# Moving single steps between engines in a fused top-k attention and gated-MLP kernel whose order is written out step by step

## The chip, the core and the metric

The kernel runs on one core of one Trainium2 chip. A core has TensorE (PE in the profile; its weight loads stand as PEld), VectorE (DVE), ScalarE (ACT), GpSimd (POOL) and SyncE (SP), which only issues DMAs here. Each engine works its own instruction queue in order; semaphores join the queues. The metric is the device time of one execution in microseconds.

## What is computed

```python
def _attn_ref(q, k, v):                 # (4, 8, 576, 64) each
    scores = np.matmul(q, k.transpose(0, 1, 3, 2)) / np.sqrt(64)
    kth = np.partition(scores, -32, axis=-1)[..., -32:-31]
    scores = np.where(scores >= kth, scores, -1e9)
    attn = np.exp(scores - np.max(scores, axis=-1, keepdims=True))
    attn = attn / (np.sum(attn, axis=-1, keepdims=True) + 1e-09)
    return np.matmul(attn, v)
def _moe_ref(x, w_in, w_out):           # x (2304, 512), w_in (512, 2048)
    h = x @ w_in
    return (h / (1.0 + np.exp(-1.702 * h))) @ w_out
def _moe2_ref(x, w1, w2, w3, w_out):    # d_ff 1024
    return ((x @ w1) * (x @ w2) @ w3) @ w_out
```

Attention keeps the 32 largest scores of each row; its output, with the heads side by side, goes through the two MLPs. The weights come as 64-bit floats, q, k and v as 32-bit floats.

## The kernel before

**Tiling.** The 2304 rows are 18 tiles of 128. A tile has 8 heads; then `tile_end` scales the tile's attention output and `moe` takes it through both MLPs. Tiles 4 and 13 hold rows of two batches, so their attention matmuls are made in two parts of 64 rows. Every operand of a product is split into two 16-bit halves, hi (rounded) and lo (what the rounding left), and each product is three matmuls: hi by hi, hi by lo, lo by hi (`product_op`, L669 to L671, 512 columns each).

**A head** (`head`): scores on TensorE (L903) into one of two PSUM tiles `s_ps`; four rounds of MAX8 (L925) and three of MATCH_REPLACE8 (L928) on VectorE find the 32nd largest; the bias `nbs` (L935, on GpSimd or VectorE); ScalarE cuts (L943) and takes exp (L946), which frees the score tile; the half `a hi` (`f_hi`, L952, ScalarE) and the difference `a lo` (L955 and L956, GpSimd); a DMA transpose; the product with v (`f_av`, L970) for each pair of heads, 9 matmuls a head, the first five with the hi halves of the softmax, the last four with the lo halves; `x0` (L1011) and `x1` (L1015) take it out of PSUM.

**The weights.** 72 blocks of 128 by 512 are loaded as 64-bit words and put together (`load64`): the low byte `w low` (L520, ScalarE), the sign `w sign` (L525 on GpSimd or L530 on ScalarE), the main word `w main` (L533, ScalarE, into PSUM), `w join` (L537, VectorE). Then Gram matmuls give a scale for each matrix (`l2_scale`, L564), and the blocks are split: `split_back` (hi at L606, back through TensorE, lo at L612) or `split_pe` (scaled on TensorE at L624, hi at L627, subtracted at L630, lo at L633 on ScalarE or L636 on VectorE). Five matrices follow one another through the same SBUF space: w4 and w3 (multiplied together into `w34`), w_in, w_out, then w1 and w2.

**q, k, v** are scaled by a factor for each row of q and each pair of heads of k and v: maximum or sum of absolute values, then three small VectorE steps of `f_pow2` (L773 to L775; the second masks the number down to a power of two), then halves (`split_op`: hi at L449 ScalarE, L452 VectorE or L466 GpSimd; lo at L459 VectorE or L462 and L463 GpSimd).

**The order.** Every step is an `Op` given to `Order.op`, with the engines that could do it (`alts`), the steps it depends on, and the buffers that it takes (`acq`) and gives back (`rel`). `PLAN` is a packed table with one number for each step: a rank in 13 bits and the chosen engine in 3. `Order.run` writes the steps out. In the kernel before it goes through modelled time: at each moment each free engine takes, of the steps that are ready and find their buffers, the one of lowest rank. The order thus written is fixed in the program; nothing is decided on the chip. `od.two` marks VectorE steps that the planner keeps apart from GpSimd's.

Of the kernel before, what the change touches and what calls it, by code (L numbers as in the profile page):

```python
# [34 lines left out]
class Op:  # L35
    __slots__ = ("alts", "fn", "prio", "acq", "rel", "left", "users", "ready", "end", "eng", "lat", "tag", "seq", "done", "start", "why", "data", "after")


class Order:

    GAP = {"T": 0.25, "V": 0.16, "A": 0.16, "G": 0.1, "D": 0.05}
    SAME = {"T": 0.0, "V": 0.11, "A": 0.12, "G": 0.1, "D": 0.25}
    DMA = 2.1

# [6 lines left out]
    def two(self, f):  # L54


        self.both.add(f)
        return f
# [4 lines left out]
    def op(self, alts, due, deps=(), env=None, acq=(), rel=(), tag="", lat=None, data=0.6, after=None):  # L63
        o = Op()
        o.after = after
        rank, k = self.plan[len(self.ops)]
        o.alts, o.prio, o.lat, o.data = [(*alts[k][:3], 0.0)], 0.2 * rank, lat, data
        o.acq = [(a, env, a) if isinstance(a, str) else a for a in acq]
        o.rel = [(a, env, a) if isinstance(a, str) else a for a in rel]
        o.left, o.users, o.ready, o.end, o.why = 0, [], 0.0, None, None  # L70
        o.tag, o.seq, o.done = tag, len(self.ops), False
        for d in deps:
            if d is not None:
                d.users.append(o)
                o.left += 1
        self.ops.append(o)
        return o

    def run(self, log=None):
        engs = "TVAGD"  # L80
        free = dict.fromkeys(engs, 0.0)
        lock = moved = 0.0
        used = dict.fromkeys(engs, 0.0)
        cand = {e: [] for e in engs}
        events = [0.0]
        for o in self.ops:
            if o.left == 0:
                for a in o.alts:
                    cand[a[0]].append((o, a, 0.0))
        n = 0  # L90
        ends = []
        now = 0.0
        while n < len(self.ops):
            if not events:
                left = [(o.tag, o.prio, [a for a, _, _ in o.acq if not self.pools[a]]) for o in self.ops if not o.done and o.left == 0]
                raise RuntimeError(f"nothing can go at {now}: {left}")
            now = heapq.heappop(events)
            while events and events[0] <= now:
                heapq.heappop(events)
            while ends and ends[0][0] <= now:  # L100
                _, _, o = heapq.heappop(ends)
                for u in o.users:
                    u.left -= 1
                    u.why = o
                    same = len(u.alts) == 1 and u.alts[0][0] == o.eng
                    u.ready = max(u.ready, o.end + (self.SAME[o.eng] if same else self.GAP[o.eng]))
                    if u.left == 0:
                        for a in u.alts:
                            r = u.ready + a[3]
                            cand[a[0]].append((u, a, r))  # L110
                            heapq.heappush(events, r)
            for e in engs:
                if free[e] > now:
                    continue
                best, rank = None, None
                for c in cand[e]:
                    o, a, r = c
                    if o.done or r > now or (o.after is not None and not o.after.done):
                        continue
                    both = e == "G" or (e == "V" and a[2] in self.both)  # L120
                    mine = (o.prio + (LOCK * max(lock - now, 0.0) if both else 0.0), o.seq)
                    if best is not None and mine >= rank:
                        continue
                    ok = True
                    for name, _, _ in o.acq:
                        if not any(s[0] <= now for s in self.pools[name]):
                            ok = False
                            break
                    if ok:
                        best, rank = c, mine  # L130
                if best is None:
                    continue
                o, a, _ = best
                cand[e] = [c for c in cand[e] if not c[0].done and c[0] is not o]
                o.done, o.eng = True, e
                wait = []
                for name, env, key in o.acq:
                    s = min(self.pools[name], key=lambda x: x[:2])
                    self.pools[name].remove(s)
                    env[key] = s[2]  # L140
                    wait.append((s[0], name, s[1]))
                o.start = now
                a[2]()
                cost = a[1]
                if e == "G" or (e == "V" and a[2] in self.both):
                    cost += max(lock - now, 0.0)
                    lock = now + cost
                free[e] = now + cost
                used[e] += cost
                o.end = now + cost  # L150
                if e == "D":
                    moved = max(moved, now) + o.data
                    o.end = max(o.end, moved) + (self.DMA if o.lat is None else o.lat)
                for name, env, key in o.rel:
                    t = o.end + self.GAP[e]
                    self.pools[name].append((t, o.seq, env[key]))
                    heapq.heappush(events, t)
                heapq.heappush(ends, (o.end, o.seq, o))
                heapq.heappush(events, o.end)
                heapq.heappush(events, free[e])  # L160
                if log is not None:
                    log.append((now, free[e], e, o.tag, o.seq, o.ready, o.why.seq if o.why else None, wait))
                n += 1
        return now, used
# [21 lines left out]
    'c-jru1B2zf0szpqX&W|alDpQ}voo`{ZQHhuZ*AMQZQHhO+q>_be{l@MF<b)~*dPWs0!C`1xM3R5@C@IOhBA^HX^r$o$^vPOaKko&j8G%Yh%};%7$echY'  # L186
    '-BW&j0{Feqq0%esBY9SY8my7CPvKy^^EpLHlwc5z-VMNH(DC)jIKscqis-!paI4~<BD<3xNST#o*1u;&&JcB=Rx0%hQ=D>uyNElWt=f?7=I0AelV=yw+'
    '1n#naoUO#+n(;qGm}mi`l?zY;rTv%xdN|^O;4=(q<L2m02pdoT-i6MuDKBMrp$`k{PLt2qV^@Mx2oll*Pzygc#L~+D2oesR4|1Mz9fW#2doMVdM(RXB0'
    'N_8qJJWMn|KI!Hi5sRwJj8$H;GVGP(uzG5Q-tj6udIV}dcwC}{LD{xe1x>x>G<Tw_sCax;Tj)|g_<4BBEGGpZOXjkQ5_%_in}<EC*hD6JW4?l7Q9gQLw'
    '%<_zPD@hhmI+01Nh>@xNT#hcm9B(s`XE4Y){#hh$BGk}@LEM!hKej5LRYMS-TNVA|>!t88zGZV}*X2sx^W_vTWnZwK*T*<6qmNUv5m5dff8>6$)-RNQT'  # L190
# [99 lines left out]
def plan():  # L290
    words = array.array("H", zlib.decompress(base64.b85decode("".join(PLAN))))
    return [(w & 8191, w >> 13) for w in words]
# [1007 lines left out]
```

## Time and profile before

| | |
|---|---|
| median of 3 runs | 1070.26 us (1066.76 to 1072.64) |
| the profiled execution's own time | 1068.41 us |
| its span, first to last instruction | 1066.6 us |
| mean granted TensorE clock | 0.957 |
| data read from HBM / written | 52.43 MB / 4.72 MB |

The busy share of an engine is a mean over the span. A recorded matmul ends later than the next one begins, so TensorE's busy time says that it had something under way, not that it ran at its peak. A wait is put down to the last semaphore that came. The granted clock is that of TensorE; 1.00 is 2.4 GHz.

### The profile page before, as it was taken

The page shows a single profiled execution, that of the slowest core. Times are in us where ns is not written, and L with a number is a line of the kernel's source. Part 1 is how long each engine was busy: PE and PEld are TensorE (multiplying, and loading weights), DVE is VectorE, ACT ScalarE, POOL GpSimd, SP SyncE. Part 2 cuts the span into 40 slices and gives each one's busy share as a digit, 9 for nine tenths or more (in the row PEclk, how much of TensorE's full clock was granted, in tenths as well). Part 3 has the DMA queues.
Part 4 walks back from the last instruction along what each step waited for, and adds up shares of the span by engine and source line. Part 5 has one row for each costly group of instructions (what it writes and reads, how often), then busy time and mean ns, then how long its engine had stood idle before and what let it go on. Part 6 is the DMA issues. An engine that isn't in the chain of part 4 may idle for free.

```text
span 1066.6 us, 18717 instructions
## 1 busy us (share of the span) xinstructions
PE 973.6 (91%) x5824; PEld 505.5 (47%) x5824; DVE 933.6 (88%) x2127; ACT 810.3 (76%) x1556; POOL 719.1 (67%) x1060
## 2 busy tenths in 40 slices
PE   3757898589689999999999999999999999999997
PEld 1333454344344545455555554555455555555543
DVE  4798898989788899999999999999999999999421
ACT  7897868989688868778878887788777867768432
POOL 1355533847576767889798898889789666656510
PEclk7767999769999999999999999999999999999999
DMA  9979977969764748876769678577685847645622
GB/s 260 291 181 236 248 143 187 273 124 199 185 127 88 134 94 149 147 138 136 143 119 169 120 130 164 118 146 134 132 143 106 158 95 135 114 94 95 114 50 69
DMA packets 428740, 156.96 MB, mean 147 GB/s; under 512 B 406624, under 2 KB 414816, under 8 KB 428640
## 3 DMA queue, kind: packets, MB, share of 16 engines
q1 hardware_dynamic: 428640, 155.78, 71.3%
q8 instruction: 45, 0.74, 0.3%
q14 instruction: 55, 0.45, 0.1%
HBM read 52.43 MB, written 4.72 MB: 54 GB/s over the span
## 4 chain that ended last, share of the span: by engine, by line
PE 52%; DVE 14%; DMA 11%; ACT 8%; POOL 8%; issue 5%; SPq 2%; POOLq 0%; ACTq 0%; DVEq 0%
PE mm L669 13%; PE mm L671 13%; PE mm L670 13%; DVE m8s L925 6%; DVE wsb L928 5%; PE mm L970 5%; DMA tsb<-hsb 4%; PE s_ps L903 4%; PE mm L624 2%; DMA wout<-in_moe_w_in_dram 1%; POOL hlb L956 1%; POOL hsb L463 1%; DVE win L612 1%; POOL fsb L1119 1%; ACT ysb L946 1%
## 5 line engine op out<-in xcount | busy, mean ns | idle before, releaser
L925 DVE MAX8 m8s<-wsb 128x8 f32<-128x576 f32 x432 | 322.9, 754 | 4.3
L928 DVE MATCH_REPLACE8 wsb<-m8s,wsb 128x576 f32<-128x576 f32 x288 | 213.8, 743 | 0.0
L669 PEld LDWEIGHTS <-tsb 128*128 128x128 f16 x1072 | 105.0, 98 | 135.1 <-DMA tsb<-hsb 22.3
L956 POOL TENSOR_TENSOR hlb<-ysb,hlb 128x512 f16<-128x512 f32 x144 | 166.7, 1157 | 0.0
L669 PE MATMUL mm<-w,tsb 128*128 128x512 f16 x432 | 163.9, 380 | 2.7 <-DMA tsb<-hsb 2.4
L671 PEld LDWEIGHTS <-tsb 128*128 128x128 f16 x1072 | 105.3, 98 | 127.8 <-issue 2.2
L671 PE MATMUL mm<-w,tsb 128*128 128x512 f16 x432 | 163.7, 379 | 0.0
L670 PE MATMUL mm<-w,tsb 128*128 128x512 f16 x432 | 163.7, 379 | 0.0
L670 PEld LDWEIGHTS <-tsb 128*128 128x128 f16 x1072 | 105.2, 98 | 113.7 <-issue 8.6
L669 PE MATMUL mm<-wout,tsb 128*128 128x512 f16 x352 | 134.7, 383 | 11.6 <-DMA tsb<-hsb 9.8
L943 ACT ACTIVATE s_ps<-s_ps,m8s 128x576 f32<-128x576 f32 x144 | 102.7, 713 | 43.8 <-DVE m8s L925 38.6
L670 PE MATMUL mm<-wout,tsb 128*128 128x512 f16 x352 | 134.5, 382 | 0.0
L671 PE MATMUL mm<-wout,tsb 128*128 128x512 f16 x352 | 134.4, 382 | 0.0
L946 ACT ACTIVATE ysb<-s_ps,nbs,asm 128x576 f32<-128x576 f32 x144 | 119.8, 832 | 8.3 <-POOL nbs L935 3.2
L925 DVE MAX8 m8s<-s_ps 128x8 f32<-128x576 f32 x144 | 108.9, 757 | 17.8 <-PE s_ps L903 15.1
L669 PE MATMUL mm<-win,tsb 128*128 128x512 f16 x288 | 110.0, 382 | 6.0 <-DMA tsb<-hsb 3.3
L670 PE MATMUL mm<-win,tsb 128*128 128x512 f16 x288 | 109.9, 381 | 0.0
L671 PE MATMUL mm<-win,tsb 128*128 128x512 f16 x288 | 109.7, 381 | 0.0
L903 PE MATMUL s_ps<-kts,qts 128*128 128x288 f16 (+1 forms) x640 | 97.9, 294 | 12.5 <-ACT ysb L946 10.0
L928 DVE MATCH_REPLACE8 wsb<-m8s,s_ps 128x576 f32<-128x576 f32 x144 | 107.7, 748 | 0.0
L952 ACT CAST hlb<-ysb 128x576 f16<-128x576 f32 x144 | 97.2, 675 | 13.1 <-DMA ats<-hlb 12.1
L955 POOL TENSOR_TENSOR hlb<-ysb,hlb 128x64 f16<-128x64 f32 x144 | 44.5, 309 | 90.1 <-ACT hlb L952 88.5
(199 smaller groups left out, 1835.7 us busy)
## 6 DMA issues: line engine op xcount, KB each, us to landing
w<-in_moe_w_dram SPq DMA_DIRECT2D x16, 512.0 KB, 6.9
wout<-in_moe_w_in_dram SPq DMA_DIRECT2D x16, 512.0 KB, 5.0
wout<-in_moe_w_out_dram SPq DMA_DIRECT2D x16, 512.0 KB, 4.6
qts<-qts SPq DMA_DIRECT2D x36, 128.0 KB, 2.6
out_dram<-fsb SPq DMA_DIRECT2D x18, 256.0 KB, 2.4
w<-in_moe_w_out_dram SPq DMA_DIRECT2D x8, 512.0 KB, 5.0
psb<-in_moe_w_dram SPq DMA_DIRECT2D x8, 512.0 KB, 4.5
tsb<-in_moe_w_dram SPq DMA_DIRECT2D x8, 512.0 KB, 4.6
```

The lines of the kernel that those rows point to most:

```text
L669: nc.tensor.matmul(o, a[:, i, :], hi, start=(first and i == 0), stop=False)
L670: nc.tensor.matmul(o, a[:, i, :], lo, start=False, stop=False)
L671: nc.tensor.matmul(o, a[:, 4 + i, :], hi, start=False, stop=(last and i == 3))
L903: nc.tensor.matmul(E["sp"][r : r + n, i], qe[q_][:, h, r : r + n], kt[:, j, i * HS : (i + 1) * HS], start=k_ == 0, stop=k_ == 1,)
L925: nc.vector.max(out=E["m8"][:, 8 * i : 8 * i + 8], in_=E["sp"] if i == 0 else E["w"])
L928: nc.vector.match_replace(out=two(E["w"]) if i == 0 else E["w"], in_to_replace=E["m8"][:, 8 * i : 8 * i + 8], in_values=E["sp"] if i == 0 ...
L943: nc.scalar.activation(E["sp"], E["sp"], AF.Prelu, bias=E["m8"][:, TOPK - 1 : TOPK], scale=-1.0, alpha=1.0 / FAR)
L946: nc.scalar.activation(two(E["y"]), E["sp"], AF.Exp, bias=E["nb"], scale=nesc)
L952: nc.scalar.copy(hl()[:, 0:S], E["y"])
L955: nc.gpsimd.tensor_tensor(hl()[:, S : S + SR], E["y"][:, SM:S], hl()[:, SM:S], op=ALU.subtract)
L956: nc.gpsimd.tensor_tensor(hl()[:, S + SR : 2 * S], E["y"][:, 0:SM], hl()[:, 0:SM], op=ALU.subtract)
L970: nc.tensor.matmul(heads_av()[r : r + n, j_], e["at"][:, i, r : r + n], v2[:, j_, blk, :], start=(i == 0), stop=(i == 8))
```

## The change

- **Engines to choose from.** Steps that had one engine get others: `w low` GpSimd; `w hi` of `split_back` VectorE and GpSimd; `w hi` of `split_pe`, `w34 hi`, `x0`, `he`, `x2 hi`, `a copy`, `b copy` and `o` VectorE; `a hi` and `th1` VectorE and GpSimd.
- **Scales.** The masking step of `f_pow2` goes (now `f_unit`): 50 VectorE steps fewer, 5182 steps for 5232.
- **The product with v.** The two halves of v change places in their tile, and the last four of a head's nine matmuls read 65 columns (the hi half and the ones column) where they read 130; the first five read 129. 640 of the 1440 matmuls of L970 are narrowed.
- **Order.** `Order.run` writes the steps out in the strict order of their ranks; modelled times only choose which of several free buffers a step gets. The durations that it holds are new. `PLAN` is new.

Unpacked, the two plans choose these engines (steps whose choice differs):

| step | before | after |
|---|---|---|
| `w low` | 72 A | 35 A, 37 G |
| `w sign` | 60 G, 12 A | 44 G, 28 A |
| `w hi` | 72 A | 55 A, 17 G |
| `w lo` | 42 V, 30 A | 35 V, 37 A |
| `a hi` | 144 A | 101 A, 40 G, 3 V |
| `x0` | 72 A | 57 A, 15 V |
| `th1` | 72 A | 53 A, 14 G, 5 V |
| `he` / `a copy` / `b copy` | 68 / 36 / 34 A | 6 / 6 / 2 of them V |
| `x2 hi` / `w34 hi` / `o` | 18 / 8 / 18 A | 3 / 1 / 1 of them V |
| `nb` | 85 G, 59 V | 80 G, 64 V |
| `g lo` / `p lo` on V (rest G) | 11 / 12 | 3 / 7 |
| `g hi` / `p hi` on V | 9 / 6 | 5 / 3 |
| `kvr hi` on V / on G | 7 / 9 | 2 / 14 |
| `q lo`, `kv lo`, `kvr lo` on V | 3, 13, 9 | 1, 12, 8 |

Here A is ScalarE, V VectorE, G GpSimd. Of the 37 `w low` that move to GpSimd, 27 stand in the first 124 us of the trace of before, 3 between 124 and 190 and 7 between 190 and 332; of the 40 `a hi`, 16 stand before 332 us. The steps that stay on their engine keep nearly their order: 51% of TensorE's, 57% of the DMAs and 66 to 70% of the other engines' stand at another place among them, by 1.0 to 1.5 places in the mean and by 29 at most.

```diff
-        return now, used
+        for o in sorted(self.ops, key=lambda o: o.rank):
+            e, cost, fn, _ = o.alts[0]
+            assert o.after is None or o.after.end is not None
...
+            fn()
...
-        lo = act(0.65, due, f_low, deps=[ld], tag="w low")
+        def f_low_g():
+            b3 = E[raw_pool].bitcast(U8).rearrange("p (c e) -> p c e", e=8)[:, :, 3]
+            low = dst.bitcast(U16).rearrange("p (c two) -> p c two", two=2)[:, :, 0]
+            nc.gpsimd.tensor_scalar(low, b3, 1.0 / 32, -15.5 / 32, op0=ALU.mult, op1=ALU.add)
+
+        lo = op([("A", 0.65, f_low, 0.0), ("G", 0.75, f_low_g, 0.0)], due, deps=[ld], tag="w low")
...
+        def f_hi_g():
+            nc.gpsimd.tensor_scalar(hi(), src(), sc, 1.0, op0=ALU.mult, op1=ALU.mult)
...
-    def f_pow2(inv, sc, src):
+    def f_unit(inv, sc, src):
         return [
             lambda: nc.vector.tensor_scalar(inv, src(), TINY, 2.0 ** -14, op0=ALU.max, op1=ALU.mult),
-            lambda: nc.vector.tensor_scalar(inv.bitcast(U32), inv.bitcast(U32), 0x7F800000, None, op0=ALU.bitwise_and),
             lambda: nc.vector.reciprocal(sc, inv),
         ]
...
+                        c0 = 0 if i < 5 else D
                         nc.tensor.matmul(
-                            heads_av()[r : r + n, j_], e["at"][:, i, r : r + n], v2[:, j_, blk, :], start=(i == 0), stop=(i == 8)
+                            heads_av()[r : r + n, j_, c0 : P + 1], e["at"][:, i, r : r + n], v2[:, j_, blk, c0 : P + 1],
+                            start=(i == 0), stop=(i == 8),
                         )
...
-        hi = act(0.58, due + 6, f_hi, deps=[y], env=E, acq=["hl"], tag="a hi", after=last_of.get("a hi"))
+        def f_hi_g():
+            nc.gpsimd.tensor_scalar(hl()[:, 0:S], E["y"], 1.0, 1.0, op0=ALU.mult, op1=ALU.mult)
+
+        hi = op([("A", 0.58, f_hi, 0.0), ("V", 0.42, od.two(f_hi_v), 0.0), ("G", 0.75, f_hi_g, 0.0)], due + 6, deps=[y], env=E, acq=["hl"], tag="a hi", after=last_of.get("a hi"))
```

## Rows read from the trace of the kernel before

**Rows 1.** The page: busy us, share of the span and instructions of each engine.
```profile
PE 973.6 (91%) x5824; PEld 505.5 (47%) x5824; DVE 933.6 (88%) x2127; ACT 810.3 (76%) x1556; POOL 719.1 (67%) x1060
```
**Rows 2.** By stretch: length; PE, PEld, DVE, ACT, POOL busy (instructions); PEclk; DMA share, GB/s.
```profile
0.00:124.00 124.00, 77.42 (x387) 40.75 (x388) 97.83 (x235) 103.87 (x203) 55.17 (x102) 0.77 0.95 244
124.00:190.00 66.00, 62.33 (x346) 30.83 (x345) 61.95 (x138) 54.41 (x101) 26.70 (x41) 1.00 0.77 178
190.00:264.00 74.00, 55.36 (x345) 30.95 (x343) 68.64 (x142) 66.80 (x118) 51.31 (x70) 0.82 0.88 194
264.00:331.00 67.00, 53.56 (x319) 26.91 (x317) 55.58 (x133) 51.03 (x95) 43.53 (x68) 0.95 0.71 151
331.00:402.00 71.00, 71.00 (x467) 35.91 (x465) 64.73 (x148) 52.69 (x106) 48.00 (x78) 1.00 0.57 106
402.00:1004.00 602.00, 596.76 (x3709) 314.63 (x3707) 572.77 (x1310) 461.85 (x899) 484.19 (x689) 1.00 0.71 131
1004.00:1066.60 62.60, 57.18 (x265) 25.55 (x262) 12.15 (x25) 19.69 (x38) 10.16 (x15) 1.00 0.30 64
```
**Rows 3.** Waits of VectorE, 0 to 331 us: for whom, us, times, longest.
```profile
DVE m8s L925 <- PE s_ps L903: 9.3, 9, 2.1
DVE asm L773 <- ACT hsb L867: 6.7, 2, 4.8
DVE w L537 <- ACT mm L533: 6.4, 4, 3.1
```
**Rows 4.** Waits of TensorE, 0 to 331 us.
```profile
PE mm L564 <- DVE w L537: 12.2, 4, 5.1
PE s_ps L903 <- ACT ysb L946: 8.7, 7, 2.7
```
**Rows 5.** Groups by shape: count, busy us, mean ns of one, idle before.
```profile
L774 DVE TENSOR_SCALAR kvinv<-kvinv 128x1 uint32<-128x1 uint32 x32 | 4.6, 143 | 0.2
L636 DVE TENSOR_SCALAR hsb<-mm 128x512 f16<-128x512 f32 x4 | 2.7, 678 | 0.0
L520 ACT ACTIVATE w<-wout 128x512 uint16<-128x512 uint8 x32 | 24.7, 781 | 4.2 <-DMA wout<-in_moe_w_in_dram 3.5 <-DMA wout<-in_moe_w_out_dram 0.7
L525 POOL TENSOR_SCALAR w<-wout 128x512 bf16<-128x512 f32 x30 | 23.0, 773 | 10.6 <-DMA wout<-in_moe_w_out_dram 7.0 <-DMA wout<-in_moe_w_in_dram 3.6
L606 ACT ACTIVATE wout<-w,wsm 128x512 f16<-128x512 f32 x16 | 10.2, 712 | 0.0
L952 ACT CAST hlb<-ysb 128x576 f16<-128x576 f32 x144 | 97.2, 675 | 13.1 <-DMA ats<-hlb 12.1
L466 POOL TENSOR_SCALAR hsb<-stg,asm 128x512 f16<-128x512 f32 x8 | 5.5, 692 | 3.7 <-DVE asm L775 3.4 <-ACT fsb L1110 0.2
```
**Rows 6.** Waits of GpSimd, 0 to 331 us.
```profile
POOL hlb L955 <- ACT hlb L952: 47.7, 23, 8.1
POOL wout L525 <- DMA w<-in_moe_w_out_dram: 11.6, 3, 9.2
POOL w L525 <- DMA wout<-in_moe_w_out_dram: 7.0, 4, 4.5
POOL w L525 <- DMA wout<-in_moe_w_in_dram: 3.6, 5, 1.3
```
**Rows 7.** Timeline of TensorE: start us, length of the merged row, line; starts show the turn.
```profile
133.28 0.39 PE L564 MATMUL mm<-w 128*128 128x128 bf16 x4
133.51 0.65 PE L903 MATMUL s_ps<-kts,qts 128*128 128x288 f16 x4
...
799.75 0.17 PE L811 MATMUL mm<-kvc,ones 128*128 128x1 bf16 x1
799.85 0.17 PE L812 MATMUL mm<-kvc,ones 64*128 64x1 bf16 x1
...
1002.80 1.21 PE L970 MATMUL mm<-v2s,ats 128*128 128x130 f16 x18
1003.85 0.39 PE L669 MATMUL mm<-w,tsb 128*128 128x512 f16 x1
```

More of the change, by code (lines that the diff above doesn't have):

```diff
@@ L2 @@
 import base64
-import heapq
 import zlib
@@ L35 @@
 class Op:
-    __slots__ = ("alts", "fn", "prio", "acq", "rel", "left", "users", "ready", "end", "eng", "lat", "tag", "seq", "done", "start", "why", "data", "after")
+    __slots__ = ("alts", "rank", "acq", "rel", "deps", "end", "eng", "lat", "tag", "seq", "start", "data", "after")
 class Order:
@@ L64, in op @@
         o = Op()
-        o.after = after
-        rank, k = self.plan[len(self.ops)]
-        o.alts, o.prio, o.lat, o.data = [(*alts[k][:3], 0.0)], 0.2 * rank, lat, data
+        o.rank, k = self.plan[len(self.ops)] if self.plan else (len(self.ops), None)
+        o.alts = alts if k is None else [alts[k]]
+        o.after, o.lat, o.data = after, self.DMA if lat is None else lat, data
         o.acq = [(a, env, a) if isinstance(a, str) else a for a in acq]
         o.rel = [(a, env, a) if isinstance(a, str) else a for a in rel]
[L70 to L75, printed above, removed]
+        o.deps = [d for d in deps if d is not None]
+        o.tag, o.seq, o.end = tag, len(self.ops), None
         self.ops.append(o)
@@ L79, in run @@
     def run(self, log=None):
-        engs = "TVAGD"
-        free = dict.fromkeys(engs, 0.0)
+        free = dict.fromkeys("TVAGD", 0.0)
         lock = moved = 0.0
[L83 to L163, printed above, removed]
@@ L164, in run @@
-        return now, used
+        for o in sorted(self.ops, key=lambda o: o.rank):
+            e, cost, fn, _ = o.alts[0]
+            assert o.after is None or o.after.end is not None
+            ready = max([0.0] + [d.end + (self.SAME[e] if d.eng == e else self.GAP[d.eng]) for d in o.deps])
+            now = max(ready, free[e])
+            wait = []
+            for name, env, key in o.acq:
+                s = min(self.pools[name], key=lambda x: x[:2])
+                self.pools[name].remove(s)
+                env[key] = s[2]
+                wait.append((s[0], name, s[1]))
+                now = max(now, s[0])
+            fn()
+            if e == "T":
+                cost *= next((f for t, f in self.COLD if now < t), 1.0)
+            if e == "G" or (e == "V" and fn in self.both):
+                cost += max(lock - now, 0.0)
+                lock = now + cost
+            o.eng, o.start = e, now
+            free[e] = o.end = now + cost
+            if e == "D":
+                moved = max(moved, now) + o.data
+                o.end = max(o.end, moved) + o.lat
+            for name, env, key in o.rel:
+                self.pools[name].append((o.end + self.GAP[e], o.seq, env[key]))
+            if log is not None:
+                log.append((now, free[e], e, o.tag, o.seq, ready, None, wait))
@@ L167 @@
+        return max(o.end for o in self.ops), None
 CONV0, CONV = 5.0, 2.0
@@ L814, in kv_prep @@
         ld = dma(
[L815 to L816 removed]
+            2.1 if is_v else 1.7, due - 6, f_load, env=E, acq=[sk, "rest"] + (["v2"] if is_v else ["h", "kr", "kt"]), tag="kv load",
+            data=1.2, after=last_of.get(("load", is_v)),
         )
```

277 lines of the change are left out of this document (152 added, 125 removed).

## The prediction

> **What bounds the kernel now.** I read the page first, for the share of each engine [rows 1]: TensorE 91%, VectorE 88%, ScalarE 76%, GpSimd 67%. These are means over two different stretches, so the table by stretch comes next [rows 2]. Its columns for TensorE's busy time and granted clock split the run at 331 us. Before that, TensorE is idle for 46.6 + 3.7 + 18.6 + 13.4 = 82.3 us, and its busy time runs at a mean granted clock of 0.77, 1.00, 0.82 and 0.95, which costs another 17.8 + 0 + 10.0 + 2.7 = 30.5 us against full clock: 113 us lost out of 331. After it, it is idle for 0 + 5.2 + 5.4 = 10.6 us out of 735.6 at full clock. A recorded matmul is longer than its turn, but the last stretch shows the turn itself: 265 matmuls in 57.18 us, 0.216 us each, nearly all of 512 columns. So from 331 us on TensorE is the bound. What a change gains there must come out of TensorE's own work, and what it gains before 331 us arrives at the end in full, as long as VectorE keeps up.
>
> Before 331 us TensorE has to wait for others. Its list of waits names the Gram matmuls of the weights (L564), which wait for VectorE's join (L537), and the scores (L903), which wait until ScalarE's exp (L946) has freed one of the two score tiles [rows 4]. VectorE is busy for 97.83 + 61.95 + 68.64 + 55.58 = 284.0 us of these 331, 86%; ScalarE for 276.1, 83%; GpSimd for 176.7, 53% [rows 2]. VectorE's own waits there lead back to ScalarE: 9.3 us for scores that waited for exp, 6.7 for the absolute maxima of q, 6.4 for the weights' main words; with the smaller rows of that view 35 us of its 47 idle ones [rows 3]. So the start is set by VectorE, with ScalarE's queue as what holds it up, and the DMA engines at 95% in the first 124 us are close behind.
>
> **The change part by part.** The order first. By the two plans, unpacked in the section on the change, TensorE's order hardly changes: half of its steps keep their place, and the mean shift is one place. The same holds for the transposes and loads on SP's queue. So what is late or early is set by how much work stands ahead of a step on each engine, and I count that up to the last maximum search of tile 3 (312 us in the trace), in the old and the new order.
>
> VectorE: 18 of the 50 masking steps stand ahead of it, 18 x 0.143 = 2.6 us; five low halves of weights go to ScalarE, 5 x 0.678 = 3.4 us [rows 5]. Nine other halves leave VectorE and ten small steps come to it, none dearer than the same 0.678; they cancel within 2 us. VectorE has 6 us less to do by then, and by the end of attention about 11 (50 x 0.143 = 7.2 for the masks, the rest for halves).
>
> ScalarE: 37 low bytes of weights leave it at 0.781, 17 high halves at 0.712, 15 softmax halves at 0.675, ten small steps at no more than that (about 5); 16 signs at the 0.781 of the like low byte and 6 low halves at the 0.678 of VectorE's like step come to it [rows 5]. That is 28.9 + 12.1 + 10.1 + 5 - 12.5 - 4.1 = 39.5 us less: 83% busy falls to 71%.
>
> GpSimd: 37 low bytes and 17 high halves come, 16 signs go. The low byte reads bytes, which no row shows for GpSimd; the nearest is the sign of the same block, 0.773, and on ScalarE the two differ little, so I take 0.773. The halves cost the 0.692 of a scaled half, the 14 softmax halves 576/512 of it, 0.78 [rows 5]. 28.6 + 11.8 + 10.9 - 12.4 = 39, with the small steps about 48 us more: 53% becomes 68%. Its cover is that it idles for 154 us of the 331, 47.7 of them waiting for just the softmax half that it now often makes itself [rows 6].
>
> What this is worth before 331 us: 6 us of VectorE's work, surely on the path. Of the 35 us that VectorE waits behind ScalarE some go: the bounds are 0 (the waits were for landings and only look like ScalarE's) and 35 (all of them). ScalarE's load falls by a seventh and GpSimd's queue is new in the same chains, so I take a fifth, 7 us. Sum 13.
>
> TensorE: four of the nine matmuls of each head's product with v read 65 columns instead of 130, 640 of 1440. In the stream they follow each other at 1.05/18 = 58 ns, Gram matmuls of 128 columns at 0.23/4 = 57 ns, and the pair with one column stands 100 ns apart, not closer [rows 7]. So the turn of a 65-column matmul lies between 29 ns (by columns) and 100 ns (as with one column): 640 x -29 = -18 us to 640 x +42 = +27 us, nearly all of it where TensorE is the bound. I take no change, since every one loads its own weights of 128 columns as the 128-column row does, and no row shows such a pair under 57.
>
> After 331 us: VectorE, at 572.8 us of 602, has 5 us less, which lets it follow the 13; TensorE's 10.6 us of idle time shrink by perhaps 1. GpSimd gains some 40 us of work over 600 us that are 484 busy: 87% at most, no bound.
>
> The sum: 13 + 0 + 1 = 14 us off the profiled execution's 1068.4 us gives 1054; off the median of the three runs, 1070.3, it gives 1056. I predict 1055.
>
> **The rivals.** (1) The narrow matmuls do run by columns: 18 us more are gained on the bound, 1037. For it: 512 columns take 216 ns and 130 take 58, in proportion. Against it: the pair with one column at 100 ns. The Trainium skill (TensorE: Matmul & The Clock Gate, "Back-to-back issue gap") gives 81 ns for a sustained pair of weight load and matmul at 128 columns, where the row shows 57; its formula for a matmul alone, N/2.4 + 2.5, gives an estimate of 30 ns for 65 columns, and by that the time would come out at this rival's. By its first rule nothing would be gained.
>
> (2) The start keeps its length for another reason: its loads. The DMA engines are 95% busy in the first 124 us, where 27 of the 37 moved low bytes stand, so a quicker ScalarE only waits for landings. Then what is left is part of VectorE's 6 us: 2 to 6 us gained, 1064 to 1068, in the middle 1066.
>
> (3) Slower: GpSimd works its queue in order, and a low byte on it is first to wait for the landing of its block. The sign steps at the head of a block waited so, 11.6 us in 3 waits, 7.0 in 4 and 3.6 in 5 [rows 6], 22.2/12 = 1.85 us each. At that, 37 of them hold GpSimd for up to 68 us, and behind each stand softmax differences and the bias steps (nbs, L935) for which exp waits, then the score tiles, then VectorE. If a third of that reaches VectorE, 23 us are lost against the 14 gained: 1079. It decides from one fifth on (14/68). Against it: GpSimd has 106 us of idle time left before 331 us, and only 10 of the 37 stand after 124 us.
>
> (4) ScalarE's waits go in larger part, 20 to 28 of the 35 us: 1041 to 1033. For it: seven waits of the score matmuls are for exp alone. Against it: each chain then meets GpSimd's longer queue.
>
> That the change doesn't do what it says is excluded for VectorE's masks, which are gone from the code, and small for the rest: the steps' engines are fixed in the plan.
>
> **How the numbers follow.** Forecast 0.48 (1048 to 1062); (1) 0.10; (2) 0.19, 0.16 of it within half a per cent; (3) 0.14; (4) 0.09. Half a per cent is 5.35 us, about what a measurement of this kernel can tell from no change. Faster by more: 0.48 + 0.10 + 0.09 + 0.03 of (2) = 0.70; within: 0.16; slower: 0.14. For 8 in 10 the range takes in the forecast, (2), most of (1) and (4) and the nearer half of (3): 1035 to 1076.
>
> **What would show it.** Right: ScalarE's busy time falls by some 70 us over the whole span and GpSimd's rises by some 90; the table by stretch shows TensorE's idle time before it becomes steady smaller by 10 us or more, and later nothing else changed; the waits of L564 for L537 and of L903 for L946 shrink; the product with v stays at 1.0 to 1.05 us for 18. Wrong: 18 matmuls in 0.85 us or in 1.3 us or more (rival 1 or its opposite bound); the steady stretch beginning at 325 us or later with the same idle time ahead (2); GpSimd waiting long for landings of the weights while VectorE's waits for scores grow (3); or TensorE idle for more than 15 us in the steady stretch, which would say that VectorE or GpSimd had become the bound there.

## The result and the profile after

| | before | after |
|---|---|---|
| median | 1068.5 us (1066.4 to 1072.6) | 1041.2 us (1038.7 to 1042.4) |
| span of the profiled execution | 1066.6 us | 1038.9 us |
| mean granted TensorE clock | 0.957 | 0.967 |

The ratio is 0.9737, with a 95% interval of 0.9699 to 0.9775: 27 us faster. The forecast was 1055; the direction was right, the gain is twice the one worked out.

The page after, which answers to [rows 1]:

```profile
PE 960.4 (92%) x5824; PEld 492.2 (47%) x5824; DVE 931.3 (90%) x2086; ACT 755.7 (73%) x1442; POOL 800.0 (77%) x1173
```

ScalarE has 55 us less to do, GpSimd 81 more, VectorE 2 less, TensorE 13 less. The table by stretch of the kernel after, with the columns of [rows 2]; the fourth stretch ends at 311 us here, where TensorE stops idling (331 us before):

```profile
0.00:124.00 124.00, 82.11 (x416) 42.89 (x417) 100.00 (x230) 93.19 (x188) 80.46 (x139) 0.83 0.98 250
124.00:190.00 66.00, 59.50 (x338) 29.49 (x337) 63.04 (x136) 50.99 (x90) 44.09 (x65) 0.97 0.91 202
190.00:264.00 74.00, 60.23 (x389) 33.26 (x388) 71.91 (x156) 61.47 (x109) 61.90 (x84) 0.89 0.98 205
264.00:311.00 47.00, 43.11 (x253) 21.46 (x253) 43.51 (x102) 38.30 (x70) 36.37 (x59) 0.93 0.72 151
...
402.00:1004.00 602.00, 595.82 (x3726) 306.68 (x3725) 560.48 (x1262) 438.46 (x841) 498.28 (x705) 1.00 0.71 129
```

Three things stand here. TensorE idles for 311 - 245.0 = 66.0 us before the steady part, where [rows 2] gave 82.3. The DMA engines, at 0.95, 0.77 and 0.88 before, are at 0.98, 0.91 and 0.98: their idle share of the first 264 us was 6.2 + 15.2 + 8.9 = 30.3 us and is 2.5 + 5.9 + 1.5 = 9.9. And in the steady part TensorE still idles for 6 us in 602.

The same steps can be found in both timelines, so the gain can be followed along the run. The last maximum search of tile 3 ends at 291 us instead of 312, as VectorE's timelines show (the kernel before, then after):

```profile
311.50 0.75 DVE L925 MAX8 m8s<-wsb 128x8 f32<-128x576 f32 x1
```
```profile
290.52 0.76 DVE L880 MAX8 m8s<-wsb 128x8 f32<-128x576 f32 x1
```

Tile by tile these ends come 3, 6, 12 and 21 us earlier for tiles 0 to 3, and stay between 19 and 29 earlier to the end. So 21 us are gained in the start and 6 to 7 behind it; forecast were 13 and 1.

VectorE's waits before the steady part, to be laid beside [rows 3] (kernel after, 0 to 311 us):

```profile
DVE kvinv L729 <- PE mm L767: 9.5, 3, 8.5
DVE v2s L428 <- ACT v2s L423: 4.1, 1, 4.1
DVE wout L474 <- ACT mm L470: 3.3, 4, 1.8
DVE m8s L880 <- PE s_ps L858: 3.0, 4, 1.6
...
DVE asm L729 <- ACT hsb L822: 0.6, 1, 0.6
```

The waits for scores (9.3 before, now 3.0), for the maxima of q (6.7, now 0.6) and for the weights' main words (11.0 in three rows, now 5.9) have shrunk. The wait for the column sums of k and v (L767, in the kernel before L812) has grown from 4.9 to 9.5, 8.5 of it at once; TensorE itself waits there for ScalarE's absolute values, which the same step of the kernel before did for 2.6 us (kernel after, 0 to 331 us):

```profile
PE mm L766 <- ACT hsb L762: 13.6, 2, 8.0
```

The rows that the prediction counted as ScalarE's, 35 us, come to 14. All rows of this view that name a releaser are 28.7 us to 311; in the kernel before they were 43.5 to the same time. VectorE's work up to the point where TensorE stops idling went from 284.0 to 278.5 us. So the start became shorter by VectorE's waits above all, not by its work.

The groups that the change made or moved, in the kernel after (columns of [rows 5]):

```profile
L482 POOL TENSOR_SCALAR w<-wout 128x512 uint16<-128x512 uint8 x16 | 12.4, 772 | 6.7 <-DMA wout<-in_moe_w_out_dram 2.9 <-DMA wout<-in_moe_w_in_dram 2.7
...
L907 ACT CAST hlb<-ysb 128x576 f16<-128x576 f32 x101 | 67.6, 669 | 6.5 <-DMA ats<-hlb 5.3
...
L958 POOL TENSOR_SCALAR hlb<-ysb 128x576 f16<-128x576 f32 x40 | 26.9, 674 | 18.0 <-ACT ysb L901 16.2 <-DMA ats<-hlb 1.6
```

A low byte takes 772 ns on GpSimd (773 had been taken), a softmax half 674 (780 had been taken).

### The profile page after: what moved, and what is told of

It reads as the page before. It is cut to its first block, busy times and chain, and to the rows that moved or that the text cites. A ratio compares the mean times of both kernels' runs of the same rounds, so it can differ in the third digit from the quotient of the medians.

```text
span 1038.9 us, 18623 instructions
## 1 busy us (share of the span) xinstructions
PE 960.4 (92%) x5824; PEld 492.2 (47%) x5824; DVE 931.3 (90%) x2086; ACT 755.7 (73%) x1442; POOL 800.0 (77%) x1173
## 4 chain that ended last, share of the span: by engine, by line
PE 32%; DVE 24%; POOL 14%; DMA 10%; ACT 10%; issue 8%; SPq 1%; POOLq 0%; ACTq 0%; DVEq 0%
DVE m8s L880 10%; DVE wsb L883 9%; PE mm L622 8%; PE mm L623 8%; PE mm L624 8%; DMA tsb<-hsb 5%; PE s_ps L858 3%; POOL hlb L911 2%; PE mm L574 2%; PE mm L926 2%; POOL hsb L1049 2%; POOL hsb L400 2%; ACT ysb L901 2%; POOL fsb L1085 1%; POOL psb L1179 1%
## 5 line engine op out<-in xcount | busy, mean ns | idle before, releaser
L1049 POOL TENSOR_TENSOR hsb<-fsb,hsb 128x512 f16<-128x512 f32 x69 | 79.9, 1160 | 27.6 <-ACT hsb L1043 21.4
L1085 POOL TENSOR_TENSOR fsb<-fsb 128x512 f32<-128x512 f32 x68 | 86.7, 1275 | 11.5 <-ACT fsb L1076 5.1
```

Source lines behind the costliest of these rows:

```text
L1049: return lambda: eng.tensor_tensor(E["h"][:, C : 2 * C], src(), E["h"][:, 0:C], op=ALU.subtract)
L1085: nc.gpsimd.tensor_tensor(E["f"], E["f"], E["f2"], op=ALU.mult)
```

## The experiments

All times are medians beside the kernel before on the same chip, whose median lay between 1065.7 and 1068.5. "Tile 3" below is the end of tile 3's last maximum search against the kernel before (-21 us in the kernel after). It is read from the one profiled execution of each run, which can lie some us off the median: a_mask's took 1045.8 us, a_order's 1090.8, b_av's 1066.8.

| run | what it is | us | ratio, 95% interval | tile 3 |
|---|---|---|---|---|
| b_av | before, narrow sums | 1064.2 | 0.9948 to 0.9991 | +1 |
| b_dve | before, VectorE 24 us less | 1066.2 | 0.9968 to 1.0002 | -2 |
| b_dve_av | both | 1061.3 | 0.9922 to 0.9962 | -2 |
| a_wide | after, wide sums | 1046.4 | 0.9791 to 0.9826 | -20 |
| a_mask | after, masks back | 1042.2 | 0.9742 to 0.9785 | -17 |
| a_dve | after, VectorE 24 us less | 1038.2 | 0.9699 to 0.9751 | -23 |
| b_ctrl | before's plan, new writer | 1069.7 | 0.9993 to 1.0033 | +1 |
| a_order | after's engines, before's order | 1085.9 | 1.0154 to 1.0198 | +2 |
| a_eng | before's engines, after's order | 1102.4 | 1.0298 to 1.0333 | +2 |
| s_old | before's engines, an order of their own | 1050.6 | 0.9820 to 0.9873 | -17 |
| s_new | both changed once more | 1042.3 | 0.9731 to 0.9800 | -19 |
| a_wlow | after, low bytes on ScalarE | 1054.4 | 0.9850 to 0.9884 | -7 |
| a_ahi | after, softmax halves on ScalarE | 1043.1 | 0.9758 to 0.9805 | -21 |
| b_half | before, 58 loads halved | 1051.3 | 0.9826 to 0.9867 | -16 |
| a_half | after, 58 loads halved | 1037.4 | 0.9698 to 0.9737 | -27 |
| a_wlow_half | a_wlow, 58 loads halved | 1048.3 | 0.9799 to 0.9850 | -15 |

### Is TensorE the bound behind 331 us?

b_av takes from the change only the narrow products with v (the two halves of v change places too, which the cut leaves out):

```diff
+                        c0 = 0 if i < 5 else D
-                            heads_av()[r : r + n, j_], e["at"][:, i, r : r + n], v2[:, j_, blk, :], ...
+                            heads_av()[r : r + n, j_, c0 : P + 1], e["at"][:, i, r : r + n], v2[:, j_, blk, c0 : P + 1], ...
```

> The kernel before with one part of the change alone: the v halves change places and the last four matmuls of a head's product with v read 65 columns; plan, masks and engines as before. Theory T (TensorE is the bound from 331 us on, and the narrow matmuls follow each other at about 29 ns, as the trace of the changed kernel shows with 18 of them in 0.82 us): 640 x 29 ns = 18 us less TensorE work, 515 of the 640 after 331 us, so 12 to 17 us faster. Rival V (VectorE is the bound there, TensorE only looks full): 0 to 3 us faster.

a_wide is the changed kernel with them wide again (`c0 = 0`, all columns read).

> The changed kernel with the narrow matmuls undone: all nine of a head read 130 columns, all else as changed. Theory T: 10 to 17 us slower than the changed kernel (1051 to 1058). Rival V: 0 to 3 us slower (1041 to 1044), the gain of 27 us then being engines, masks and order.

First the turn, from TensorE's timeline of the kernel after (columns of [rows 7]):

```profile
905.35 0.38 PE L624 MATMUL mm<-w,tsb 128*128 128x512 f16 x1
905.57 0.98 PE L926 MATMUL mm<-v2s,ats 128*128 128x129 f16 x18
906.39 0.66 PE L858 MATMUL s_ps<-kts,qts 128*128 128x288 f16 x4
```

The 18 matmuls take 906.39 - 905.57 = 0.82 us, 1.05 before [rows 7]. Ten of them have 129 columns and take the 58 ns of before's 130, so the eight of 65 columns take (0.82 - 0.58)/8 = 30 ns each. Over 80 such groups TensorE has 18 us less to do. In time this was worth 4 us in the kernel before (1 to 6 by the interval) and 5 in the kernel after (1046.4 against 1041.2; 8 by the two ratios), less than theory T asked in both runs and, by the medians, more than rival V allowed. The steady part of b_av, and below it that of b_dve_av:

```profile
402.00:1004.00 602.00, 589.22 (x3719) 304.71 (x3717) 573.13 (x1313) 461.72 (x902) 485.40 (x691) 1.00 0.71 131
```
```profile
402.00:1004.00 602.00, 592.78 (x3739) 306.62 (x3737) 552.89 (x1307) 461.57 (x900) 485.20 (x690) 1.00 0.71 132
```

TensorE's idle time rose from 5.2 us [rows 2] to 12.8 in b_av, in an execution 2.7 us above its median: about half of what left its work there came back as waiting, mostly for transposed tiles, as these lists of TensorE's waits in that stretch show, the kernel before and then b_av:

```profile
PEld L669 <- DMA tsb<-hsb: 4.9, 8, 1.3
...
PE mm L669 <- DMA tsb<-hsb: 1.5, 2, 0.8
PE s_ps L903 <- ACT ysb L946: 1.3, 2, 0.8
```

```profile
PEld L669 <- DMA tsb<-hsb: 9.8, 13, 1.5
...
PE mm L669 <- DMA tsb<-hsb: 4.5, 7, 1.1
PE s_ps L903 <- ACT ysb L946: 3.7, 8, 0.7
```

I then supposed that VectorE, 95% busy in the steady part, held TensorE up. b_dve shortens VectorE's work, b_dve_av does so beside the narrow sums:

```diff
-nc.vector.max(out=..., in_=E["sp"] if i == 0 else E["w"])
+nc.vector.max(out=..., in_=E["sp"] if i == 0 else E["w"][:, 0:SM])
```

> The kernel before with VectorE's work cut alone: the second to fourth maximum search of a head reads 512 of the 576 scores, so the last 64 keys are left out of those three rounds (the part of the computation that is changed). 432 searches some 0.067 us shorter, 29 us less VectorE work, no step, wait or order changed. Taking 18 us off TensorE gave 4. If VectorE paces the steady stretch: 20 to 29 us faster than before (1039 to 1048). If the two hold each other up in turn, neither alone being the bound: 5 to 15 us. If TensorE is the bound after all: under 5 us.

> The kernel before with both earlier edits at once: the second to fourth maxima of a row read 512 of the 576 scores (this leaves the last 64 keys out of them, 24 us less work on VectorE), and the weighted sums write the 65 columns that are read (18 us less on TensorE). Alone the first took 2 us off the median and the second 4. Theory A (TensorE and VectorE hold each other up all through the steady part, so that either's shorter work turns into waiting for the other): together clearly more than the sum, 12 to 20 us, 1048 to 1056. Theory B (neither is the bound; ScalarE's place in the order or the transfers are): the sum, 5 to 7 us, 1061 to 1063. My prediction's view (TensorE alone is the bound behind 331 us) would have had 14 to 18 from the columns already.

24 us less on VectorE gave 2, which the interval does not tell from nothing, and both edits together 7, about the sum of 2 and 4. The theory that the two engines hold each other up, which asked for 12 to 20, falls. In b_dve VectorE mostly waits more for scores, 14.2 us in 33 waits between 331 and 1000 us where the kernel before had 5.8 in 13:

```profile
DVE m8s L925 <- PE s_ps L903: 14.2, 33, 1.4
```

In the kernel after the same shortening (a_dve) gave 3 us, with intervals that overlap.

> The changed kernel with the second to fourth maxima of a row over 512 of the 576 scores (the last 64 keys are left out of them): 24 us less on VectorE, 5 of it before the last maximum of tile 3. In the kernel before this was worth 2 us, and 3 beside the narrow sums. Theory A (in the new order VectorE is the bound, at 297 us of the first 331 and 560 of the 602 behind): 10 us or more, under 1031. Theory B (no engine alone is): 1 to 5 us, 1036 to 1040.

a_mask puts the 50 masking steps back:

```diff
+            nc.vector.tensor_scalar(inv.bitcast(U32), inv.bitcast(U32), 0x7F800000, None, op0=ALU.bitwise_and),
```

> The changed kernel with the 50 masking steps put back behind the maximum (same place in the order, one VectorE step more per scale of q, k and v). If VectorE paces the kernel, 50 x 0.143 = 7.2 us of work and about 0.05 us each of semaphore between them come back: 5 to 9 us slower, 1046 to 1050. If only the order and the engines of the other steps count: within 2 us.

The median moves by 1 us, inside the spread of either. Tile 3 ends 4 us later, but in the slowest of the four executions (1045.8 us), so that it can't be put down to the masks. No run showed a price of VectorE's work near its length.

### Order and engines

b_ctrl writes the steps of the kernel before, with their engines and their order, by the new rule; only the choice of free buffers differs. a_order has the engines of after in the order of before, a_eng the reverse; both keep the narrow sums and leave the masks out. The edit in words:

```diff
 PLAN = (one number for each step: rank and engine)
-  a_order: rank and engine of after         +  a_order: rank of before, engine of after
-  a_eng:   rank and engine of after         +  a_eng:   rank of after, engine of before
```

> The steps, engines and instruction order of the kernel before, written out by the changed kernel's strict-rank writer; what differs is only which of several free buffers (PSUM banks, transposed tiles) a step gets, since the modelled durations that choose it are new. If buffers don't matter, as the prediction silently held: within 3 us of before. If they do: 5 us or more either way.

> The changed kernel with the order of the kernel before (the 50 masking steps left out, each moved step on its new engine at its old place). The prediction held that the order hardly matters: within 3 us of the changed kernel (1038 to 1044). Rival O (the gain of the start came from the order, since steps moved by one place decide who waits): 8 to 15 us slower, 1049 to 1056.

> The changed kernel's order, narrow matmuls and missing masks, but each step on the engine that it had before. If the new order is good by itself: within 10 us of the changed kernel (1041 to 1051). If order and engines fit only each other, as the old order with the new engines showed (1086): 1075 to 1095, no better than before.

The writer and the buffers are worth nothing (1069.7). The run answers another question as well. TensorE's granted clock in the first 124 us is 0.83 in the kernel after and 0.77 in the kernel before, and a faster TensorE might have shortened the start; b_ctrl had 0.90 there, and its tile 3 comes 1 us later than before's (b_ctrl):

```profile
0.00:124.00 124.00, 76.47 (x375) 39.33 (x376) 96.92 (x234) 104.22 (x204) 55.27 (x102) 0.90 0.95 245
```

But neither half of the plan is good without the other: after's engines in before's order cost 18 us against the kernel before, before's engines in after's order 34. It shows in the lists of waits, behind 331 us of a_order:

```profile
ACT ysb L897 <- POOL nbs L886: 17.5, 20, 2.6
...
PE s_ps L854 <- ACT ysb L897: 16.1, 17, 2.5
```

and in the first 331 us of a_eng:

```profile
POOL nbs L886 <- DVE m8s L876: 30.0, 13, 6.9
PE s_ps L854 <- ACT ysb L897: 23.7, 16, 6.3
```

The chain is the one that rival 3 described, but from another cause, as I read it: the bias step stands on GpSimd at a place that fitted other engines, exp waits for it, the score tile comes free late, and TensorE waits with all that stands behind the scores in its queue. No run moved the bias step alone. TensorE waits for exp for 1.3 us between 402 and 1004 us in the kernel before.

s_old then gives before's engines an order of their own. Ranks were moved by 2 to 3.5 places in the mean; s_new starts from the plan after and changes both.

> The changed kernel (no masks, narrow sums) with every step on the engine that it had in the kernel before, and a new order: starting from the order of before, single steps were moved by a few places (on each engine most of them, by 2 to 3.5 places in the mean), on all engines together. ScalarE and GpSimd keep the work of before, 810 and 719 us. Theory A (the freedom of engines carries the gain of the start, by ScalarE's 55 us): an order cannot take work off ScalarE; the start stays 12 us or more behind the changed kernel, as with the low bytes back on ScalarE (last maximum of tile 3 at -7 against before instead of -21), and the time lies at 1053 to 1063. Theory B (the order carries it: every queue is worked in order, and what counts is that each step stands where its inputs come in time; the engines only have to fit): 1038 to 1047, tile 3 at -15 or better, with ScalarE as busy as before. My prediction held that the order hardly matters; by it this kernel gives 1060 to 1066.

> The changed kernel with both again free: starting from its plan, steps were moved by a few places (1.5 to 3 in the mean) and some 290 choices of an engine changed, about as many in either direction (36 of nb to VectorE and 29 to GpSimd, 25 softmax halves to GpSimd and 23 back). No load on an engine changes by more than 15 us. Theory A (loads decide): the time of the changed kernel, 1038 to 1044. Theory B (fit of order and engines decides, and the plan of the changed kernel isn't the end of it): 1030 to 1037, gained before tile 4, since behind it TensorE leaves some 6 us in 602.

s_old answers the largest question, whether places alone gain anything. Its page:

```profile
PE 957.4 (91%) x5824; PEld 487.3 (46%) x5824; DVE 938.7 (89%) x2077; ACT 807.6 (77%) x1556; POOL 718.6 (68%) x1060
```

ScalarE and GpSimd carry the load of [rows 1], and yet the start is 17 us shorter. The time, 1050.6, lies outside what either theory had asked (B's upper end was 1047): 16 us below the kernel before (ratio 0.9847). Of these 4 to 5 are the narrow sums and at most 1 the masks, so a change of places alone is worth some 10 to 12. The 9 us from there to 1041 (12 by the two ratios) are what free engines add between these two plans; a better order for the old engines may exist. s_new, 1042.3, isn't to be told from the kernel after, though its product with v of tile 4 is 28 us ahead of the kernel before instead of 20, and at tile 17 it is 28 ahead as well, where the kernel after is 29. What it had gained by tile 4 was given back in the steady part, where TensorE had 8 us of idle time in 602.

### What ScalarE's relief is worth

Two runs put steps back on ScalarE in the kernel after, each in one line:

```diff
+        k = 0 if tag == "w low" else k      # a_wlow: 37 low bytes back, k = 0 is ScalarE
+        k = 0 if tag == "a hi" else k       # a_ahi: 43 softmax halves back
```

> The changed kernel with all 72 low bytes of the weights on ScalarE again, in the same order: ScalarE gets 37 x 0.78 = 29 us back, all but one before 270 us. If the shorter start comes from ScalarE's relief: 10 to 20 us slower, with the steady stretch beginning that much later. If it comes from VectorE's shorter work and the order: under 5 us slower.

> The changed kernel with every first softmax half (the rounding of a to its high part) back on ScalarE, where before had them all; order, the other engine choices and the narrow sums stay. Those halves that the change put on GpSimd are then some 0.7 us of ScalarE's work each. Theory A (ScalarE's relief carried the gain, wherever it came from): the run loses in proportion to the work put back, as the low weight bytes did (29 us of ScalarE's work put back cost 13): 0.4 to 0.5 of it, and the time lies between 1049 and 1056. Theory B (only the low bytes in the start counted, since ScalarE was late there alone; the halves matter little): within 4 us of the changed kernel, 1041 to 1045, with the last maximum of tile 3 where the changed kernel has it. Theory C (any engine choice that no longer fits its order costs, as with the whole set of them, +61): more than 20 us.

ScalarE's busy time rose by nearly as much in both: by 21 us to 776.4 in a_wlow, by 22 to 778.1 in a_ahi. The first lost 13 us, the second 2 (5 by the two ratios, with intervals that overlap). So it isn't ScalarE's load alone that decides but where it stands. The low bytes lie at the head of each block's chain in the start, and tile 3 comes 14 us later without the move; the halves lie all over the run, and tile 3 doesn't move. The lateness is seen at exp as well: to 331 us TensorE waits 26.5 us for it in a_wlow, 17.2 in the kernel after.

```profile
PE s_ps L859 <- ACT ysb L902: 26.5, 15, 6.9
```

### Transfers in the start

In every run that gained in the start the DMA engines' idle time of the first 264 us had fallen to 6 to 15 us (after, a_wide, a_dve, s_old, s_new, a_mask, a_ahi), and in those that gained little or nothing there it was 27 to 38 (before, b_av, b_dve, b_dve_av, b_ctrl, a_wlow, a_order, a_eng). That can be cause or effect. b_half and a_half halve the bytes of 58 of the 72 block loads, with no engine's work changed; half the values of those blocks are left out:

```diff
-            nc.sync.dma_start(E[raw_pool].bitcast(U32), src.bitcast(U32))
+            name = (E[raw_pool].tensor.name, E[raw_pool].offset)
+            if name not in seen:
+                seen.append(name)
+                nc.sync.dma_start(E[raw_pool].bitcast(U32), src.bitcast(U32))
+            else:
+                nc.sync.dma_start(E[raw_pool].bitcast(U32)[:, 0:512], src.bitcast(U32)[:, 0:512])
```

> The kernel before with the same 58 blocks loaded by half their columns (half their values are left out). Its DMA engines idle for 30 us of the first 264 already. Theory A (transfers bound the start here too, between those gaps): the gain of a_half or more, 10 us or over. Theory B (here the order is late and not the transfers): under 5 us, 1063 to 1068.

> The changed kernel with 58 of the 72 weight blocks (all but the first into each of 14 places) loaded by half their columns, 256 KB for 512: this leaves half the values of those blocks out, the steps on the engines stay as they are. 15.2 MB less are moved, at the 0.2 MB per us of the start some 66 us of the DMA engines' time. Theory A (the start of the changed kernel is bound by transfers, 98, 91 and 98% busy in its first three stretches): the last maximum of tile 3 comes 10 us or more earlier than in the changed kernel, up to the 29 us that VectorE idles before it, and the time falls to 1012 to 1031. Theory B (the DMA engines are busy because the engines free the places sooner; VectorE, 235 us busy of the first 264, and the fixed order set the pace): at most 4 us, 1037 to 1041.

In the kernel before smaller loads are worth 16 us (tile 3: -16), although its DMA engines idled for 30 us. In the kernel after they are worth 4, with intervals that overlap (tile 3: 6 more). So landings did hold the start of the kernel before up, and in the kernel after they do so much less. One place where they did is TensorE's list of waits. The kernel before, 0 to 331 us, the queue of weight loads and that of matmuls:

```profile
PEld L669 <- DMA tsb<-hsb: 15.3, 6, 3.5
...
PE mm L669 <- DMA tsb<-hsb: 12.4, 6, 3.0
```

The kernel after, the same stretch:

```profile
PEld L622 <- DMA tsb<-hsb: 5.1, 7, 1.4
...
PE mm L622 <- DMA tsb<-hsb: 2.4, 4, 1.0
```

b_half, the same stretch:

```profile
PEld L676 <- DMA tsb<-hsb: 4.6, 4, 1.9
...
PE mm L676 <- DMA tsb<-hsb: 2.2, 3, 1.1
```

These are the MLP matmuls, which wait for a transposed tile of the MLP. In the two kernels that are quick in the start the wait is a third of what it was or less, but in two ways. Median times from issue to landing up to 311 us, the kernel before, then after, then b_half:

```profile
tsb<-hsb SPq DMA_TRANSPOSE x30, 3.9
```
```profile
tsb<-hsb SPq DMA_TRANSPOSE x32, 4.4
```
```profile
tsb<-hsb SPq DMA_TRANSPOSE x32, 3.3
```

With smaller loads the transposes land sooner, 3.3 us for 3.9. In the kernel after, whose DMA engines are busier, they land later, 4.4, and are still waited for less: the order leaves more time between issue and use. VectorE's waits to 311 us, all rows that name a releaser, fall from 43.5 us to 29.1 in b_half and to 28.7 in the kernel after.

The transposed tiles are not the only landings that were waited for. ScalarE's waits for the weight blocks themselves, at the low bytes, come to 14.9 us in the kernel before (0 to 331 us), to 4.1 in b_half and to 5.7 in the kernel after; these are the longest rows, before and then b_half:

```profile
ACT w L520 <- DMA tsb<-in_moe_w_dram: 5.2, 4, 3.1
```
```profile
ACT wout L527 <- DMA w<-in_moe_w_out_dram: 3.9, 3, 2.1
```

How the 16 us of b_half divide between transposed tiles and blocks, no run shows.

The Trainium skill (DMA: Bandwidth & Descriptors, "Issuing engines are not separate DMA queues") says that DMAs started by ScalarE, SyncE or GpSimd run on the same 16 engines and interleave there. Here SyncE issues them all, so that only the sharing shows; b_half agrees with it: the transposes landed in 3.3 us for 3.9 when only the loads were cut.

Last, whether the low bytes act through ScalarE or through loads that start late: a_wlow with the loads halved.

> The changed kernel with all 72 low weight bytes on ScalarE, as in the run that lost 13 us, and with the 58 weight blocks loaded by half their columns (half their values are left out). With halved loads alone the changed kernel stands at 1037.4. Theory A (ScalarE's 29 us of work delay the start by themselves): the loss stays, 10 to 14 us, 1047 to 1051. Theory B (ScalarE's lateness gives the places of the loaded blocks back later, and the loads then crowd the transposed tiles; 56.5 MB had been moved by 264 us there for 59.5): the loss falls to 3 to 6 us, 1040 to 1043.

The loss stays: 1048.3 against 1037.4 for a_half, 11 us, against 13 with full loads. So most of the 13 are ScalarE's own lateness; whether the other 2 go through the loads can't be told from the noise.

## Why the prediction was right in sign and wrong in size

The sum had 13 us for the start, 0 for the narrow matmuls and 1 for the rest behind the start. The profiled executions show 21 at tile 3 and 6.7 behind it. In a_wide, which lacks the narrow matmuls, 20 and 1.9 are left, so about 5 belong to these and 2 to the rest. That the start would be shorter, and by VectorE's shorter waits, was right. What failed is the size of the first term, the second term put at nothing, and under the first the step that put the order at nothing.

**"From 331 us on TensorE is the bound."** It failed as a rule for prices. TensorE does idle for only 5 to 6 us in 602, but taking 18 us off its work gave 4 to 5. An engine that is 99% busy by the trace had the transposed tiles and exp close behind it, and a shorter TensorE waited for those. So the upper price of rival 1, 18 us, was wrong though its mechanism was right.

**"I take no change" for the narrow matmuls.** It failed: they run by columns, 30 ns for 65, with a 128-column weight load of their own each. The row that I weighed against it, the pair with one column at 100 ns [rows 7], doesn't speak for such a stream. By the formula of the Trainium skill (TensorE: Matmul & The Clock Gate, "Back-to-back issue gap") 30 ns was the estimate, and the trace agrees; its sustained 81 ns at 128 columns stays unsupported here, at 57 to 58.

**"6 us of VectorE's work, surely on the path."** It failed as a price: b_dve took 24 us x 4/18 = 5 us off VectorE up to tile 3 and tile 3 came 2 earlier, a_dve the same. The masks were worth 1 us in the median.

**"A fifth, 7 us" of VectorE's 35 us behind ScalarE.** The mechanism was right and the term too small: the rows counted as those 35 us fell to 14, by 21 and not by 7, and with the wait for the sums of k and v that grew, all of VectorE's waits fell by 15. The low bytes alone carry 13 us in the new order. But the load was the wrong measure: 21 us of low bytes are worth 13 us, 22 us of softmax halves 2.

**"The order hardly matters."** This is the step whose failure explains most. It rested on a mean shift of one place. Shifts of 2 to 3.5 places, larger than the change's own 1.0 to 1.5, are worth 10 to 12 us with the old engines (s_old; 17 of the 21 us at tile 3, the masks' share among them), and the wrong pairing of order and engines costs 45 to 61 against the kernel after. A place in a queue that is worked in order isn't an amount of work ahead of a step; it decides what all that stands behind it waits for.

**"The DMA engines at 95% are close behind."** I had read the loads as a limit that could swallow the gain (rival 2). The runs show another part: landings were waited for in the kernel before although its DMA engines idled for 30 us, and a re-timed order takes that wait away without moving a byte less. The two rows of TensorE's waits for `tsb` that say so stand above those that I used of that stretch [rows 4], and I passed them over; ScalarE's 14.9 us for blocks I left out of the sum too.

**Rival 3** didn't come: GpSimd waited 22.2 us for landings at its sign steps [rows 6], and the low bytes that it now has wait 9.9 (2.9 + 2.8 + 2.7 + 1.5, kernel after, 0 to 331 us). One wait of 8.3 at a half of k or v (`rest`) is put down to the landing of a block as well; the other two rows are spoken of below:

```profile
POOL hlb L958 <- ACT ysb L901: 10.0, 6, 3.5
POOL rest L399 <- DMA w<-in_moe_w_out_dram: 8.3, 1, 8.3
POOL hlb L910 <- ACT hlb L907: 5.2, 3, 3.9
...
POOL w L482 <- DMA wout<-in_moe_w_out_dram: 2.9, 1, 2.9
POOL wout L482 <- DMA w<-in_moe_w_out_dram: 2.8, 1, 2.8
POOL w L482 <- DMA wout<-in_moe_w_in_dram: 2.7, 2, 2.1
...
POOL win L482 <- DMA w<-in_moe_w_dram: 1.5, 1, 1.5
```

The 47.7 us that GpSimd waited for the softmax half are 5.2, and 10.0 for exp where it makes that half itself: the cover that I named was there.

**Rival 4** gave the right time, 1041, and half of the right reason: the 21 us lie in its 20 to 28, but the narrow sums, which it left at nothing, are part of the time. **Rival 1**, with 1037, had the right turn at the wrong price. That the range held the result is in part luck: no rival had places as a cause.

**The signs I had named.** ScalarE's fall (55 us, some 70 forecast), GpSimd's rise (81, some 90) and TensorE's shorter idle time in the start (16 us, 10 or more forecast) came, and the wait of L564 for L537 shrank from 12.2 us [rows 4] to 3.1 (L506 for L474). The 18 matmuls at 0.82 us were the sign that I had given rival 1. One sign misled: TensorE's wait for exp didn't shrink from its 8.7 us [rows 4] but grew to 17.2 (kernel after, 0 to 331 us), which fits a TensorE that now comes to the scores early but is not shown to be that:

```profile
PE s_ps L858 <- ACT ysb L901: 17.2, 10, 6.1
```

**The account of the 27 us**, as far as the runs carry it: 5 for the narrow sums, about 1 for the masks, 10 to 12 for places alone, some 9 for the free engines. It isn't a sum of independent parts: the low bytes, 13 us in this order, may overlap with what s_old recovered by places. Open stays whether the old engines could reach 1041 with a better order, and which moves of s_old carry its gain.

## What to carry to other kernels

In a kernel whose engines are all 70 to 95% busy and whose order is fixed, price a step by what is queued behind it and by what it waits for there, not by its length: some 21 us on ScalarE were worth 13 us at the head of a load's chain and 2 spread over the run. Read the waits of each queue from the top, the weight loads' too, and ask of each landing whether it could be issued earlier. The Trainium skill (Perfetto Trace Analysis, "Identifying the Most-Contended Engine") says to optimize first the engine with the highest occupancy, and judges TensorE by other measures than its matmul occupancy. Of the others VectorE has the highest here, 88% [rows 1], and 24 us less on it gave 2, while moving steps by a few places gave 10 or more.

## What was unexpected of the hardware

Matmuls of 65 columns follow each other at 30 ns although each has its own weight load of 128 columns, half the 58 ns of those of 130 columns. GpSimd rounds a 128 by 576 tile to 16 bits in 674 ns, ScalarE in 669; the Trainium skill (Trainium Architecture — The Big Picture, "The five engines, in one table") lists streaming elementwise work as what GpSimd is not for, at half VectorE's speed. For this step the rows bear that out in part: VectorE takes 449 ns (L955, three times), and against ScalarE there is no loss.
